# A layer of two decode attentions on one core: the first half of B's output weights loaded to 64 partitions in eight small transfers, and the last exp placed ahead of the product before it

## The chip, the cores and the metric

The kernel runs on one core of a Trainium2 chip. The metric is device time in microseconds (us), the median of three runs. One of the executions was taken by the hardware profiler; all rows and times below that are not called runs are from that one. Its times count from the first instruction of the span.

## What is computed

Two attention blocks, A and B, of the same shape, each for one query token. In each, a row x (512) is multiplied with wq (512 x 4096) to give 32 heads of 128; each head is scored against its own 8192 cached keys, goes through a softmax, and is multiplied with its 8192 cached values; the 32 results are laid end to end (4096) and multiplied with wo (4096 x 512). The two rows of 512 are put side by side.

```
q = (x @ wq).reshape(B, Sq, H, Dh).transpose(0, 2, 1, 3)
scores = einsum("bhqd,bhkd->bhqk", q, k_cache) * (Dh ** -0.5)
p = softmax(scores)
o = einsum("bhqk,bhkd->bhqd", p, v_cache)
y = o.transpose(0, 2, 1, 3).reshape(B, Sq, H * Dh) @ wo
out = concatenate([y of A, y of B], axis=-1)
```

All is bf16. The caches are 64 heads x 8192 x 128 x 2 bytes, twice: 268 MB. With wq and wo of both blocks (4 MB each) the kernel reads 285 MB.

## The kernel before

The work goes in **32 pairs of heads** (n = 0 to 31; 0 to 15 are A's, 16 to 31 B's). One pair has its two heads on 128 partitions: head one's 8192 positions on partitions 0 to 63, head two's on 64 to 127, 128 positions to a partition. So the keys of a pair are one transfer of 4 MB, 128 partitions x 32 KB, and so are the values.

`load_k` and `load_v` issue these transfers from SyncE's queue (SP) into two buffers each (`kn`, `vn`). A load into a buffer waits on SP until the pair that had it is through: keys of pair n wait for `red_done[n-2]`, values for `pv_done[n-2]`. The keys of pair 31 and the values of pair 31 come in four quarters.

For one pair: VectorE multiplies the keys with the query, in four pieces (`plan_mul`, L265). TensorE sums over the head dimension by 32 matmuls with an identity (`plan_red`, L274), VectorE adds the rest (`plan_sr`, L283) and takes each partition's maximum (`plan_max`, L289). `plan_gmax` brings the maxima into one row by a matmul (tile `mtp`, L295), and VectorE reduces them (L298). `plan_exp` spreads the maximum back to the partitions by four small matmuls (tile `bmp`, L308), and ScalarE makes `negb` of it (L312) and then the two exps (L319), which also leave the row sums. `plan_sum` adds the row sums by a matmul into the tile `misc` (L330; for the last three pairs L337) and takes the reciprocal. `plan_pv` multiplies with the values: 32 matmuls of 512 columns (L359), or, for the last three pairs (n >= MV = 29), 128 matmuls of 2 columns (L354), whose result `plan_o` scales straight into `oD` (L378).

The program's order is written out by hand: one Python loop over n calls these functions, and every engine carries out its own instructions in the order of the calls. In iteration n the steps of pair n up to its exp are mixed with the values product of pair n-2 (for the last three pairs, n-1).

**The output projection of B.** `oD` holds the heads with the head dimension on the partitions. `WOG` cuts the heads in groups; for each, `plan_relayout` (L414, L418, L420) turns the heads of the group into a layout in which partition p has rows of wo that lie side by side in memory, so that a group's part of wo is loaded in long runs: VectorE multiplies with a mask into `zb`, TensorE multiplies with `jsel` into `misc`, VectorE copies it out. `misc` is one tile, used in turn by the sums, by `plan_o` and by the relayouts; each use waits for the use before it. `plan_wot` (L441) then adds, for each group, four matmuls per row of wo, accumulating in `qyp`; `plan_yt` copies, transposes and casts the result (L454, L455, L457), and the last DMA writes it.

For B the groups are heads 0 to 15, 16 to 23, 24 to 27, 28 and 29, 30 and 31. The first, 2 MB on 128 partitions x 16 KB, is loaded in iteration 24. The other four, 2 MB together, are issued in iteration 31 behind the quarters of the values of pair 31, the last of the big transfers. All of wo lies in `wbuf`, which held wq and A's wo before.

```
            if n == 24:
                load_wo(1, 0)
            if n == NP - 1:
                for g in range(1, len(WOG[1])):
                    load_wo(1, g)
...
                plan_gmax(n)
                if ahead:
                    plan_mul(n + 1, 1)
                if n > MV:
                    plan_pv(n - 1, 0, T)
                plan_exp(n)
```

So in iteration 31 TensorE has, in this order: the matmuls of L295 for pair 31, the 128 matmuls of pair 30's values (L354), the matmuls of L308 for the exp of pair 31, the relayout product of heads 28 and 29 (L418), and from iteration 32 the sum of pair 31 (L337), the values product of pair 31 in four quarters, and the groups of the projection.

Of the kernel before, what the change touches and what calls it, by code (L numbers as in the profile page):

```python
# [6 lines left out]
ALU = mybir.AluOpType  # L7
AX = mybir.AxisListType
BF16 = mybir.dt.bfloat16
F32 = mybir.dt.float32  # L10

P = 128
# [11 lines left out]
class _Plan:  # L24
# [15 lines left out]
    def op(self, eng, fn, ctr=None, needs=(), inc=1):  # L40

        for m in needs:
            self.wait(eng, m)
        if ctr is None:
            self.prog[eng].append(fn)
            return None
        ctr.n += inc
        self.prog[eng].append(lambda e: fn(e).then_inc(ctr.sem, inc))
        return ctr, ctr.n


def bass_concat_heads__mha_block_cached__gqa_block_cached__decode_kernel(
# [17 lines left out]
    wos = [A_wo, B_wo]  # L70
    NA = 2
    H, Sk, Dh = ks[0].shape[1:]
    D = xs[0].shape[2]
    NOUT = wos[0].shape[1]
# [5 lines left out]
    T = Sk // HP  # L80
    assert T == 128
    PA = H // 2
    NP = NA * PA
    NK = NV = 2
# [3 lines left out]
    DW = 512 // HT  # L88
    assert Dh % DW == 0

    WOG = [[(0, 32)], [(0, 16), (16, 8), (24, 4), (28, 2), (30, 2)]]
    RG = [32, 16, 8, 4, 2]

    MV = NP - 3

    with ExitStack() as st:
# [3 lines left out]
        def sb(name, shape, dt):  # L100
            return ec(nc.sbuf_tensor(name, shape, dt))

        kn = sb("kn", [P, NK, T, Dh], BF16)
        vn = sb("vn", [P, NV, T, Dh], BF16)
        wbuf = sb("wbuf", [P, C * H * Dh], BF16)
        wq_sb = wbuf[:].rearrange("p (c n) -> p c n", c=C)
        wo_sb = wbuf[:].rearrange("p (j n) -> p j n", n=NOUT)
        qbc = sb("qbc", [P, NP, Dh], BF16)

        pt = sb("pt", [P, 2, T // 4, 8], BF16)  # L110
# [15 lines left out]
        rinv = sb("rinv", [P, NP, 2], F32)  # L126
        oD = sb("oD", [P, NA, H], BF16)
        zb = sb("zb", [P, 2, P], BF16)
        o2 = sb("o2", [P, NA, H], BF16)
        mask = {g: sb("mask%d" % g, [P, P // g], BF16) for g in RG}  # L130
        jsel = {g: sb("jsel%d" % g, [P, g], BF16) for g in RG}
        out_sb = sb("out_sb", [1, NOUT], BF16)
        NQ = NOUT // P
# [16 lines left out]
        def ctr(name):  # L150
            return _Ctr(nc, st, name)

        s_x = ctr("s_x")
        s_w = ctr("s_w")
        s_wo = [ctr("s_wo%d" % i) for i in range(5)]
        s_part = {(x, i): ctr("s_%s_part%d" % (x, i)) for x in "kv" for i in range(1, 4)}
        s_k = [ctr("s_k%d" % i) for i in range(NK)]
        s_v = [ctr("s_v%d" % i) for i in range(NV)]
# [4 lines left out]
        def dma(eng, dst, src, c, needs=()):  # L163
            return op(eng, lambda e: e.dma_start(dst, src), c, needs, inc=16)
# [50 lines left out]
            wq_in[a] = dma("SP", wbuf[:], wqs[a].rearrange("(p c) n -> p (c n)", p=P), s_w,  # L215
                           [q_done.get(a - 1)])

        def load_wo(a, g):
            h0, n = WOG[a][g]
            src = wos[a][h0 * Dh:(h0 + n) * Dh, :].rearrange("(p j) n -> p (j n)", p=P)  # L220
            wo_in[a, g] = dma("SP", wo_sb[:, h0:h0 + n, :].rearrange("p j n -> p (j n)"), src, s_wo[g],
                              [q_done[NA - 1] if a == 0 else wo_done[0]])


        for a in range(NA):
# [78 lines left out]
        def plan_exp(n):  # L304
            def bc(e):
                r = None
                for h in range(2):
                    r = e.matmul(bmp[:, 0:1], hrow[0:1, h, :], gm[0:1, n, h:h + 1],  # L308
                                 start=(h == 0), stop=(h == 1))
                return r  # L310
            m = op("PE", bc, c_pe, [i_pool, gm_done[n], nb_done.get(n - 1)])
            nb_done[n] = op("ACT", lambda e: e.activation(  # L312
                negb[:, n:n + 1], bmp[:, 0:1], AF.Copy, scale=-scale), c_act, [m])
            wait("ACT", nb_done[n])
            wait("ACT", pv_done.get(n - 2))
            wait("ACT", i_pool)
            for h in range(2):
                q = slice(h * HP, (h + 1) * HP)
                p_done[n] = op("ACT", lambda e, h=h, q=q: e.activation(  # L319
                    pt[q, n % 2, :, 4 * h:4 * h + 4],  # L320
                    s_sb[q, n % 2, :].rearrange("p (c t) -> p c t", t=4), AF.Exp,
                    bias=negb[q, n:n + 1], scale=scale, accum_out=rsum[q, n, h:h + 1]), c_act)
# [83 lines left out]
        o2_ready = {}  # L406

        def plan_relayout(a, g):
            h0, n = WOG[a][g]
            z = z_n[0] % 2  # L410
            z_n[0] += 1
            s = P // n
            zv = zb[:, z, :].rearrange("p (h s) -> p h s", s=s)
            m = op("DVE", lambda e: e.tensor_tensor(  # L414
                zv, oD[:, a, h0:h0 + n].unsqueeze(2).broadcast_to([P, n, s]),
                mask[n][:, None, :].broadcast_to([P, n, s]), ALU.mult),
                c_dve, [sel_ready[n], o_done[a * PA + (h0 + n) // 2 - 1], z_free.get(z)])
            z_free[z] = op("PE", lambda e: e.matmul(misc[:, 0:n], zb[:, z, :], jsel[n][:],  # L418
                                                    start=True, stop=True), c_pe, [m, misc_free[0]])
            o2_ready[a, g] = misc_free[0] = op("DVE", lambda e: e.tensor_copy(  # L420
                o2[:, a, h0:h0 + n], misc[:, 0:n]), c_dve, [z_free[z]])

        def plan_wo(g, j0, j1):

            def mm(e):
                r = None
                for j in range(j0, j1):
                    r = e.matmul(qyp[0:1, :], o2[:, 0, j:j + 1], wo_sb[:, j, :],  # L428
                                 start=(j == 0), stop=(j == H - 1))
                return r  # L430
            wo_done[0] = op("PE", mm, c_pe, [o2_ready[0, g], wo_in[0, g]] + ([qy_free[0]] if j0 == 0 else []))

        def plan_wot(g):

            h0, n = WOG[1][g]

            def mm(e):
                r = None
                for j in range(h0, h0 + n):
                    for i in range(NQ):  # L440
                        r = e.matmul(qyp[:, i:i + 1], wo_sb[:, j, i * P:(i + 1) * P],  # L441
                                     o2[:, 1, j:j + 1], start=(j == 0 and i == 0),
                                     stop=(j == H - 1 and i == NQ - 1), skip_group_check=True)
                return r
            wo_done[1] = op("PE", mm, c_pe, [o2_ready[1, g], wo_in[1, g], qy_free[0]])

        y_done = {}
# [17 lines left out]
        for n in range(NP + 1):  # L465
            last = n == NP

            ahead = n == NP - 2
            if n + 1 < NP:
                load_k(n + 1, 4 if ahead else 1)  # L470
            if 0 < n < NP:
                plan_sum(n - 1)
            if n < NP - 1:
                plan_mul(n, 0)
                plan_mul(n, 1)
            if 1 < n <= MV + 1:
                plan_pv(n - 2, 0, T)
                plan_ac(n - 2)
            if not last:
                load_v(n, 4 if n == NP - 1 else 1)  # L480
            if n == 0:
                load_wq(1)
            if n == 12:
                load_wo(0, 0)
            if n == 24:
                load_wo(1, 0)
            if n == NP - 1:
                for g in range(1, len(WOG[1])):
                    load_wo(1, g)
            if not last:  # L490
                plan_red(n, 0)
            if n < NP - 1:
                plan_mul(n, 2)
                plan_mul(n, 3)
            if not last:
                plan_sr(n, 0)
            if 1 < n <= MV + 1:
                plan_o(n - 2)
            if not last:
                plan_red(n, 1)  # L500
                plan_sr(n, 1)
                plan_max(n)
                if ahead:
                    plan_mul(n + 1, 0)
                plan_gmax(n)
                if ahead:
                    plan_mul(n + 1, 1)
                if n > MV:
                    plan_pv(n - 1, 0, T)
                plan_exp(n)  # L510
            else:
                plan_sum(n - 1)
                for i in range(4):
                    plan_pv(n - 1, i * T // 4, (i + 1) * T // 4)
                plan_wot(1)
            if n > MV:
                plan_o(n - 1)
            if 3 <= n < 7:
                plan_q(1, n - 3)
            if n == PA + 1:  # L520
                plan_relayout(0, 0)
            if PA + 1 < n <= PA + 5:
                plan_wo(0, 8 * (n - PA - 2), 8 * (n - PA - 1))
                if n == PA + 5:
                    plan_y()
            for g, (h0, k) in enumerate(WOG[1]):
                p = (h0 + k) // 2 + PA - 1
                if n == (p + 2 if p < MV - 1 else p + 1):
                    plan_relayout(1, g)
            if n == 28:  # L530
                plan_wot(0)
            if ahead:
                plan_mul(n + 1, 2)
                plan_mul(n + 1, 3)
        for g in range(2, len(WOG[1])):
            plan_wot(g)
        plan_yt()
        dma("SP", out[0, :, 0:NOUT], out_sb[:], s_out, [y_done[0]])
# [38 lines left out]
```

## Time and profile before

| what | value |
|---|---|
| runs before | 674.28 us median (674.13 to 674.54), three runs |
| the profiled execution | 674.46 us; its span 672.4 us |
| TensorE matmul busy | 554.5 us, 82% of the span |
| VectorE busy | 358.9 us, 53% |
| ScalarE busy | 63.6 us, 9% |
| read from HBM | 285.21 MB, 424 GB/s over the span |
| mean granted TensorE clock | 0.913 of full speed |

The profile is read in views. The page gives busy times, the span in 40 slices (with the busy share of the 16 DMA engines), the DMA queues, and groups of instructions. The chain of waits is followed back from the last instruction to what released each step. The timeline lists instructions with their starts, durations and the idle time before them. The windows give busy times between two moments. The trace behind the views also holds every DMA packet with its start, duration and size, and every semaphore event; where a number below is counted from these, the text says so.

### The profile page before, as it was taken

How to read it: one execution, taken by the hardware profiler on the slowest of the kernel's cores; microseconds unless marked ns; L12 is line 12 of the kernel's file. 1: busy time of each engine (PE TensorE's matmuls, PEld its weight loads, DVE VectorE, ACT ScalarE, POOL GpSimd, SP SyncE). 2: the span in 40 equal slices, each digit the busy share in tenths (PEclk: the TensorE clock that was granted, in tenths of full speed). 3: DMA queues.
4: the chain of work that ended last, by engine and by line, in shares of the span. 5: the costliest groups of instructions: out<-in, count | busy, mean ns of one | idle time of the engine just before them, and what ended most of it. 6: DMA issues, size and time to landing. Idle time of an engine off the chain costs nothing.

```text
span 672.4 us, 6851 instructions
## 1 busy us (share of the span) xinstructions
PE 554.5 (82%) x3006; PEld 233.2 (35%) x3006; DVE 358.9 (53%) x345; ACT 63.6 (9%) x200; POOL 2.6 (0%) x17
## 2 busy tenths in 40 slices
PE   2657799989888889874888899999889888798986
PEld 1223333333333333331333333333333333343345
DVE  1563456565455665615655556565545664456561
ACT  1101010111011001110110110111010111010000
POOL 1000000000000000000000000000000000000000
PEclk9969999898889998896898999988789988899876
DMA  9999999999999999999999999999999999999996
GB/s 374 437 436 433 432 425 424 435 434 433 432 432 425 432 435 432 431 428 437 425 430 434 431 430 435 430 427 434 426 433 436 431 426 431 430 433 434 415 423 256
DMA packets 11275, 285.65 MB, mean 425 GB/s; under 512 B 1259, under 2 KB 1262, under 8 KB 1646
## 3 DMA queue, kind: packets, MB, share of 16 engines
q1 hardware_dynamic: 11242, 285.22, 98.9%
q8 instruction: 23, 0.38, 0.2%
q14 instruction: 6, 0.05, 0.0%
q10 hardware_dynamic: 4, 0.00, 0.0%
HBM read 285.21 MB, written 0.00 MB: 424 GB/s over the span
## 4 chain that ended last, share of the span: by engine, by line
PE 57%; DMA 28%; DVE 9%; issue 3%; ACT 2%; SPq 0%
PE rps L274 26%; PE acc L359 24%; DMA kn<-in_A_k_cache_dram 16%; DMA kn<-in_B_k_cache_dram 8%; DVE kn L265 5%; DMA wbuf<-in_B_wo_dram 3%; DVE s_sb L283 2%; PE bmp L308 2%; ACT pt L319 2%; PE mtp L295 1%; PE qyp L428 1%; DVE m L289 1%; DVE gm L298 1%; PE misc L330 1%; PE misc L386 1%
## 5 line engine op out<-in xcount | busy, mean ns | idle before, releaser
L265 DVE TENSOR_TENSOR kn<-kn,qbc 128x4096 bf16<-128x4096 bf16 x128 | 284.7, 2284 | 84.2 <-DMA kn<-in_A_k_cache_dram 61.2
L274 PE MATMUL rps<-kn,ident 128*128 128x512 bf16 x1024 | 240.5, 390 | 24.2 <-DVE kn L265 24.2
L359 PE MATMUL acc<-vn,pt 128*8 128x512 bf16 x928 | 236.4, 419 | 0.0
L274 PEld LDWEIGHTS rps<-kn,ident 128*128 128x128 bf16 x1024 | 97.6, 100 | 152.2 <-issue 25.4
L359 PEld LDWEIGHTS acc<-vn,pt 128*8 128x8 bf16 x928 | 84.9, 93 | 137.5 <-issue 45.9
L283 DVE TENSOR_REDUCE s_sb<-rps 128x64 f32<-128x512 f32 x64 | 44.2, 691 | 126.5 <-PE rps L274 126.5
L371 ACT ACTIVATE accsb<-acc,rinv 8x512 bf16<-8x512 f32 x29 | 19.7, 678 | 244.5 <-PE acc L359 244.5
L295 PE MATMUL mtp<-ident_f,m 128*1 128x128 f32 x64 | 12.1, 271 | 35.3 <-DVE m L289 35.3
L334 DVE RECIPROCAL rinv<-misc 8x1 f32<-8x1 f32 x29 | 4.5, 155 | 64.9 <-PE misc L330 64.9
L312 ACT ACTIVATE negb<-bmp 128x1 f32<-128x1 f32 x32 | 5.5, 171 | 332.0 <-PE bmp L308 332.0
L330 PE MATMUL misc<-rsum,hind 128*8 128x1 f32 x116 | 7.2, 166 | 26.3 <-ACT pt L319 26.3
L308 PE MATMUL bmp<-gm,hrow 1*128 1x1 f32 x128 | 19.6, 253 | 11.2 <-DVE gm L298 11.2
L319 ACT ACTIVATE pt<-s_sb,negb 64x128 bf16<-64x128 f32 x64 | 25.5, 399 | 1.8
L308 PEld LDWEIGHTS bmp<-gm,hrow 1*128 1x128 f32 x128 | 16.9, 189 | 20.0 <-DVE gm L298 19.3
L295 PEld LDWEIGHTS mtp<-ident_f,m 128*1 128x1 f32 x64 | 2.7, 81 | 51.1 <-DVE m L289 51.1
L247 PE MATMUL qyp<-wbuf,xb 128*64 128x512 bf16 x64 | 13.7, 571 | 6.4 <-DMA wbuf<-in_A_wq_dram 4.3
L298 DVE TENSOR_REDUCE gm<-mtp 1x2 f32<-1x128 f32 x32 | 8.9, 278 | 14.6 <-PE mtp L295 14.6
L330 PEld LDWEIGHTS misc<-rsum,hind 128*8 128x8 f32 x116 | 4.8, 90 | 32.3 <-ACT pt L319 30.6
L319 ACT ACTIVATION_READ_ACCUMULATOR pt<-s_sb,negb 64x1 f32 x64 | 11.8, 185 | 0.0
L428 PE MATMUL qyp<-wbuf,o 128*1 128x512 bf16 x32 | 10.7, 494 | 0.0
L354 PEld LDWEIGHTS acc<-pt,vn 128*128 128x128 bf16 x384 | 10.3, 99 | 0.4 <-issue 0.4
L354 PE MATMUL acc<-pt,vn 128*128 128x2 bf16 x384 | 10.3, 164 | 0.0
(48 smaller groups left out, 65.6 us busy)
## 6 DMA issues: line engine op xcount, KB each, us to landing
kn<-in_A_k_cache_dram SPq DMA_DIRECT2D x16, 4096.0 KB, 26.1
vn<-in_A_v_cache_dram SPq DMA_DIRECT2D x16, 4096.0 KB, 23.7
kn<-in_B_k_cache_dram SPq DMA_DIRECT2D x15, 4096.0 KB, 25.5
vn<-in_B_v_cache_dram SPq DMA_DIRECT2D x15, 4096.0 KB, 23.0
wbuf<-in_A_wq_dram SPq DMA_DIRECT2D x1, 4096.0 KB, 12.3
wbuf<-in_B_wq_dram SPq DMA_DIRECT2D x1, 4096.0 KB, 30.3
wbuf<-in_A_wo_dram SPq DMA_DIRECT2D x1, 4096.0 KB, 32.6
kn<-in_B_k_cache_dram SPq DMA_DIRECT2D x4, 1024.0 KB, 21.2
```

The source lines that it names most:

```text
L265: mul_done[n, c] = op("DVE", lambda e: e.tensor_tensor(k, k, qbc[:, n:n + 1, :].broadcast_to([P, CT, Dh]), ALU.mult), c_mul, [k_in[n][c * ...
L274: r = e.matmul(rps[:, h, :].rearrange("p (t d) -> p t d", d=DW), ident[:], kn[:, n % NK, h * HT:(h + 1) * HT, i * DW:(i + 1) * DW], start= ...
L283: sr_done[n, h] = op("DVE", lambda e: e.tensor_reduce(s_sb[:, n % 2, h * HT:(h + 1) * HT], rps[:, h, :].rearrange("p (t d) -> p t d", d=DW ...
L295: m = op("PE", lambda e: e.matmul(mtp[0:1, 0:P], m1[:, n:n + 1], ident_f[:], start=True, stop=True), c_pe, [m_done[n], i_identf, gm_done.g ...
L298: gm_done[n] = op("DVE", lambda e: e.tensor_reduce(gm[:, n, :], mtp[0:1, 0:P].rearrange("o (h p) -> o h p", h=2), AX.X, ALU.max), c_dve, [m])
L308: r = e.matmul(bmp[:, 0:1], hrow[0:1, h, :], gm[0:1, n, h:h + 1], start=(h == 0), stop=(h == 1))
L319: p_done[n] = op("ACT", lambda e, h=h, q=q: e.activation(pt[q, n % 2, :, 4 * h:4 * h + 4], s_sb[q, n % 2, :].rearrange("p (c t) -> p c t", ...
L330: r = e.matmul(misc[0:8, 0:1], hind[:], rsum[:, n, h:h + 1], start=(h == 0), stop=(h == 1))
L354: r = e.matmul(acc[:, n % 2, 0:2], vn[:, n % NV, t, :], pt[:, n % 2, t // 4, t % 4:8:4], start=(t == 0), stop=(t == T - 1))
L359: r = e.matmul(acc[0:8, n % 2, :], pt[:, n % 2, c, :], vn[:, n % NV, 4 * c:4 * c + 4, :].rearrange("p t d -> p (t d)"), start=(c == 0), st ...
L371: ac_done[n] = op("ACT", lambda e: e.activation(accsb[:, n % 2, :], acc[0:8, n % 2, :], AF.Copy, scale=rinv[0:8, n, 0:1]), c_act, [pv_done ...
L428: r = e.matmul(qyp[0:1, :], o2[:, 0, j:j + 1], wo_sb[:, j, :], start=(j == 0), stop=(j == H - 1))
```

## The change

Five things are edited.

- **Groups of B.** Heads 0 to 15 become two groups. `WOG` now holds (first head, heads, rows of wo to a partition): heads 0 to 7 with 16 rows to a partition, which fill partitions 0 to 63, and heads 8 to 15 with 8 rows on 128 partitions. The four groups of the tail are as before.
- **Their loads.** Heads 0 to 7 (1 MB) are loaded by eight DMAs of 8 partitions x 16 KB each; DMA i takes the partitions b, b+4, ..., b+28 with b = 32*(i // 4) + i % 4. Two of the eight are issued in each of the iterations 22 to 25, behind the loads of that iteration. Heads 8 to 15 (1 MB, 128 partitions x 8 KB) follow in iteration 26. The load in iteration 24 is gone.
- **The tail's loads** are the same four transfers at the same place in SP's queue, but go into the `kn` buffer that pair 30's keys had, and wait for `red_done[30]` instead of `wo_done[0]`.
- **Relayout and projection** get one group more: one mask product, one matmul and one copy, and in iteration 28 a second `plan_wot` of 32 matmuls. The results `o2` are one tensor for each group.
- **The exp of pair 31** is called ahead of the values product of pair 30, so TensorE has L308 of pair 31 ahead of the 128 matmuls of L354 of pair 30. The iterations before keep their order.

```diff
-    WOG = [[(0, 32)], [(0, 16), (16, 8), (24, 4), (28, 2), (30, 2)]]
+    WOG = [[(0, 32, 32)], [(0, 8, 16), (8, 8, 8), (16, 8, 8), (24, 4, 4), (28, 2, 2), (30, 2, 2)]]
+        wo_kn = kn[:, NP % NK].rearrange("p t d -> p (t d)").rearrange("p (j n) -> p j n", n=NOUT)
...
-        def load_wo(a, g):
-            h0, n = WOG[a][g]
-            src = wos[a][h0 * Dh:(h0 + n) * Dh, :].rearrange("(p j) n -> p (j n)", p=P)
-            wo_in[a, g] = dma("SP", wo_sb[:, h0:h0 + n, :].rearrange("p j n -> p (j n)"), src, s_wo[g],
-                              [q_done[NA - 1] if a == 0 else wo_done[0]])
+        def wo_rows(a, g):
+
+            h0, n, r = WOG[a][g]
+            if a == 0 or g < 2:
+                return n * Dh // r, wo_sb, 16 if (a, g) == (1, 1) else 0
+            return P, wo_kn, h0 - WOG[1][2][0]
+
+        def load_wo(a, g, parts=range(8)):
+            h0, n, r = WOG[a][g]
+            np_, tile, j0 = wo_rows(a, g)
+            src = wos[a][h0 * Dh:(h0 + n) * Dh, :].rearrange("(p j) n -> p (j n)", p=np_)
+            dst = tile[0:np_, j0:j0 + r, :].rearrange("p j n -> p (j n)")
+            need = [q_done[NA - 1]] if a == 0 else [wo_done[0]] if g < 2 else [red_done[NP - 2]]
+            if np_ == P:
+                wo_in[a, g] = dma("SP", dst, src, s_wo[g], need)
+                return
+
+            for i in parts:
+                b = 32 * (i // 4) + i % 4
+                wo_in[a, g] = dma("SP", dst[b:b + 29:4, :], src[b:b + 29:4, :], s_wo[g], need)
...
-            if n == 24:
-                load_wo(1, 0)
+            if 22 <= n < 26:
+                load_wo(1, 0, range(2 * (n - 22), 2 * (n - 21)))
+            if n == 26:
+                load_wo(1, 1)
             if n == NP - 1:
-                for g in range(1, len(WOG[1])):
+                for g in range(2, len(WOG[1])):
                     load_wo(1, g)
...
-                if n > MV:
+                if n > MV and n < NP - 1:
                     plan_pv(n - 1, 0, T)
                 plan_exp(n)
+                if n == NP - 1:
+                    plan_pv(n - 1, 0, T)
             else:
                 plan_sum(n - 1)
                 for i in range(4):
                     plan_pv(n - 1, i * T // 4, (i + 1) * T // 4)
-                plan_wot(1)
+                plan_wot(2)
...
             if n == 28:
                 plan_wot(0)
+                plan_wot(1)
```

More of the change, by code (lines that the diff above doesn't have):

```diff
@@ L128, in bass_concat_heads__mha_block_cached__gqa_block_cached__decode_kernel @@
         zb = sb("zb", [P, 2, P], BF16)
-        o2 = sb("o2", [P, NA, H], BF16)
+        o2 = {(a, g): sb("o2_%d_%d" % (a, g), [P, r], BF16)
+              for a in range(NA) for g, (_, _, r) in enumerate(WOG[a])}
         mask = {g: sb("mask%d" % g, [P, P // g], BF16) for g in RG}
@@ L154, in bass_concat_heads__mha_block_cached__gqa_block_cached__decode_kernel @@
         s_w = ctr("s_w")
-        s_wo = [ctr("s_wo%d" % i) for i in range(5)]
+        s_wo = [ctr("s_wo%d" % i) for i in range(6)]
         s_part = {(x, i): ctr("s_%s_part%d" % (x, i)) for x in "kv" for i in range(1, 4)}
@@ L408, in plan_relayout @@
         def plan_relayout(a, g):
-            h0, n = WOG[a][g]
+            h0, n, r = WOG[a][g]
             z = z_n[0] % 2
             z_n[0] += 1
-            s = P // n
-            zv = zb[:, z, :].rearrange("p (h s) -> p h s", s=s)
+            w = P // r
+            m_ = n * w
+            zv = zb[:, z, 0:m_].rearrange("p (h s) -> p h s", s=w)
             m = op("DVE", lambda e: e.tensor_tensor(
[L415 to L418, printed above, removed]
+                zv, oD[:, a, h0:h0 + n].unsqueeze(2).broadcast_to([P, n, w]),
+                mask[r][:, None, :].broadcast_to([P, n, w]), ALU.mult),
+                c_dve, [sel_ready[r], o_done[a * PA + (h0 + n) // 2 - 1], z_free.get(z)])
+            z_free[z] = op("PE", lambda e: e.matmul(misc[0:m_, 0:r], zb[:, z, 0:m_], jsel[r][:],
                                                     start=True, stop=True), c_pe, [m, misc_free[0]])
             o2_ready[a, g] = misc_free[0] = op("DVE", lambda e: e.tensor_copy(
-                o2[:, a, h0:h0 + n], misc[:, 0:n]), c_dve, [z_free[z]])
+                o2[a, g][0:m_, :], misc[0:m_, 0:r]), c_dve, [z_free[z]])
         def plan_wo(g, j0, j1):
@@ L427, in mm @@
                 for j in range(j0, j1):
-                    r = e.matmul(qyp[0:1, :], o2[:, 0, j:j + 1], wo_sb[:, j, :],
+                    r = e.matmul(qyp[0:1, :], o2[0, g][:, j:j + 1], wo_sb[:, j, :],
                                  start=(j == 0), stop=(j == H - 1))
@@ L433, in plan_wot @@
         def plan_wot(g):
-            h0, n = WOG[1][g]
+            h0, n, r = WOG[1][g]
+            np_, tile, j0 = wo_rows(1, g)
+            end = g == len(WOG[1]) - 1
             def mm(e):
-                r = None
-                for j in range(h0, h0 + n):
+                res = None
+                for j in range(r):
                     for i in range(NQ):
[L441 to L444, printed above, removed]
+                        res = e.matmul(qyp[:, i:i + 1], tile[0:np_, j0 + j, i * P:(i + 1) * P],
+                                       o2[1, g][0:np_, j:j + 1], start=(g == 0 and j == 0 and i == 0),
+                                       stop=(end and j == r - 1 and i == NQ - 1), skip_group_check=True)
+                return res
             wo_done[1] = op("PE", mm, c_pe, [o2_ready[1, g], wo_in[1, g], qy_free[0]])
@@ L525, in bass_concat_heads__mha_block_cached__gqa_block_cached__decode_kernel @@
                     plan_y()
-            for g, (h0, k) in enumerate(WOG[1]):
+            for g, (h0, k, _) in enumerate(WOG[1]):
                 p = (h0 + k) // 2 + PA - 1
@@ L534, in bass_concat_heads__mha_block_cached__gqa_block_cached__decode_kernel @@
                 plan_mul(n + 1, 3)
-        for g in range(2, len(WOG[1])):
+        for g in range(3, len(WOG[1])):
             plan_wot(g)
```

## The prediction

> **What bounds the kernel now.** First the page's 40 slices: the busy share of the 16 DMA engines and the bytes per second.
>
> ```profile
> DMA  9999999999999999999999999999999999999996
> GB/s 374 437 436 433 432 425 424 435 434 433 432 432 425 432 435 432 431 428 437 425 430 434 431 430 435 430 427 434 426 433 436 431 426 431 430 433 434 415 423 256
> ```
>
> The transfers never pause; only the last slice falls, to 256 GB/s. PE at 82% is not the limit. Next the page's DMA queues:
>
> ```profile
> q1 hardware_dynamic: 11242, 285.22, 98.9%
> q8 instruction: 23, 0.38, 0.2%
> q14 instruction: 6, 0.05, 0.0%
> ```
>
> Beside the kernel's loads the DMA engines fetch instructions: 23 packets of 16 KB, 6 of 8 KB. Then the end of the chain of waits (start, us, what):
>
> ```profile
> 646.64 21.85 DMA wbuf<-in_B_wo_dram
> 668.49 0.05 issue
> 668.54 0.19 PE qyp L441
> 668.73 0.42 issue
> 669.14 0.57 PE qyp L441 x15
> ```
>
> The last link is a load of wo. By the semaphore events the last group is complete at 669.13, and the last 15 matmuls start at 669.14. So the end goes one to one with the last DMA engine to finish. The windows (PEclk, DMA share, GB/s are the last three columns) show that they do not finish together:
>
> ```profile
> 655.00:663.40 8.40, 6.19 (x167) 5.24 (x166) 2.04 (x7) 1.15 (x5) 0.00 (x0) 0.86 1.01 415
> 663.40:664.90 1.50, 1.50 (x61) 1.50 (x59) 0.00 (x0) 0.00 (x0) 0.00 (x0) 0.50 0.67 275
> 664.90:666.90 2.00, 1.63 (x61) 1.55 (x59) 0.45 (x2) 0.00 (x0) 0.00 (x0) 0.50 0.58 228
> 666.90:668.40 1.50, 1.30 (x46) 1.22 (x43) 0.16 (x1) 0.00 (x0) 0.00 (x0) 0.50 0.36 141
> ```
>
> From 663.4 on a third of the engines has nothing to do. I counted this from the trace's packets and semaphore events. Each 128-partition transfer leaves 16 events, one per engine. Those of the last transfer come, after the first one, at **0, 0.06, 0.15, 0.18, 0.20, 0.77, 1.45 | 3.04, 3.35, 3.37, 4.75, 4.78, 4.83, 4.96, 5.05, 5.20 us**: seven early engines, nine late. Followed back over the transfers, all run at one pace (9.70 us for eight packets of 32 KB); a lag comes from an instruction fetch and stays. Each of the 23 large fetches puts one engine 1.56 us back (at 50 us, from 0.41 to 1.97), in turns over the same eight engines. Small ones put one other engine back 0.97 us three times: that is the 3.04.
>
> The profile's execution took 674.46 us: 672.43 of span and 2.03 around it. The median is 0.18 lower; I make the sum on 674.46 and carry the difference to 674.28.
>
> **Part 1: heads 0 to 7 in eight DMAs of 8 partitions.** Bytes in total stay. A transfer of one partition (`out_sb`) left one data packet and one 4-byte packet, the one of four (`out_q`) four of each; so I take 8 partitions for 8 engines, one packet of 16 KB each. The eight DMAs all have the same form, so I take the same eight engines for all: they carry 8 x 0.614 us (median of 16 KB packets) for these heads, and, like all, 8 x 0.313 (8 KB) for heads 8 to 15. Before, each engine had 8 x 0.614 for heads 0 to 15. The eight **receivers** get 2.50 us and eight more 4-byte packets of 9 ns, **+2.57 us**; the other eight get 8 x 0.614 less, about **-2.40**.
>
> The time of the end is the largest lag. Eight receivers among seven early engines cannot all be early: at least one of the nine late ones receives. The best choice is the one at 3.04: it ends at 3.04 + 2.57 = 5.61 where the worst was 5.20, **+0.41 us**. The six that now end at 4.75 to 5.20 go to 2.35 to 2.80 and no longer matter; the worst engine is another one, no better. If a receiver at 3.37 joins, +0.74. If one at 5.20 does, +2.57. Which eight receive? The one-partition `out_sb` ran at 663.46, just behind the earliest engine's last packet of wo, so that small-transfer engine is one of the six without fetches. This speaks for the receivers being the eight engines without large fetches, and the late one among them that at 3.04. I take +0.41.
>
> [...] The slices above show queues that never run dry, so I hold that the other eight engines go on with the next transfer.
>
> What it issues: eight instructions on SP instead of one, at 0.43 us each (the row of the wo loads), and one for heads 8 to 15: two per iteration, 0.86 us. Behind them on SP is the next load of keys, which waits for `red_done` anyway: pair 29's was issued at 579.06 and its packets began at about 590 on the earliest engine. These 11 us of queue hide it (8 for the values of pair 28, issued at 591.47, begun at 599.7); without them it would cost 0.86 us an iteration. The wait for `wo_done[0]` is over by iteration 22.
>
> Iteration 28 gets 32 matmuls more, 0.85 us (64 took 1.69 on the chain), and one more relayout (VectorE 0.27 + 0.17, PE 0.18). The engines wait for keys there (VectorE is idle 2.6 us before pair 28's product, 2.2 before pair 29's, both released by the DMA), and the same 8 to 11 us of queue cover it. The tail's loads into `kn` wait for `red_done[30]`, done before `pv_done[29]`, which SP has already waited for: nothing. PE fetches some 66 instructions more, 4 KB, a quarter of a fetch: the fetches come a little earlier, on engines that now have 2.4 us to spare.
>
> **Part 2: the exp ahead.** Rows of the timeline before:
>
> ```profile
> 657.05 3.37 PE L354 MATMUL acc<-pt,vn 128*128 128x2 bf16 x128
> 657.16 0.28 DVE L298 TENSOR_REDUCE gm<-mtp 1x2 f32<-1x128 f32 x1 [0.47 <-PE mtp L295]
> 660.35 0.60 PE L308 MATMUL bmp<-gm,hrow 1*128 1x1 f32 x4
> 660.46 0.16 DVE L378 TENSOR_TENSOR oD<-acc,rinv 128x2 bf16<-128x2 f32 x1 [3.02 <-PE acc L354]
> 661.00 0.19 PE L418 MATMUL misc<-jsel,zb 128*128 128x2 bf16 x1
> 661.22 0.16 DVE L420 CAST o<-misc 128x2 bf16<-128x2 f32 x1 [0.28 <-PE misc L418]
> 662.25 0.59 PE L337 MATMUL misc<-rsum,ones_f 128*128 128x2 f32 x2 [1.06 <-ACT pt L319]
> 662.69 3.59 PE L354 MATMUL acc<-pt,vn 128*128 128x2 bf16 x128
> ```
>
> Now L308 runs from 657.48 to 658.08, pair 30's product to about 661.4, and the exp (1.85 us from L308 to L337) is done beside it. But what is late next is the relayout of heads 28 and 29: it starts when that product ends and takes 0.96 us to its copy (660.42 to 661.38 above), and L337 must wait for this copy, as it writes the same `misc`. So L337 starts at about 662.42 and pair 31's product at 662.86 instead of 662.69: **0.17 us later**, not earlier. Between ends: if the relayout did not hold it up, it would come 0.8 us earlier. Either way the loads cover it: the values' last quarter lands by 664.6, heads 16 to 23 at 667.0, the last group at 669.54. PE alone would reach the end of its last matmuls at 667.90 + 32 x 0.032 = 668.9 against 669.71, so 0.8 us of cover. Cost 0.
>
> **Sum:** 674.46 + 0.41 = 674.87, against the median **674.7 us**.
>
> **Rivals.**
> - *Forecast, 0.71:* the end moves by the engine at 3.04 or 3.37, 674.6 to 675.1.
> - *A twice or thrice delayed fetch engine is among the receivers, 0.15:* slower. Place: the last wo transfer; price up to 2.57, 676.9; it passes 0.2% (1.35 us) from the point at which a receiver's lag before was over 3.98, and six of sixteen engines were. For: only one receiver can be told from the trace. Against: that one has no fetches, and eight fetch engines leave just eight others.
> - *The eight DMAs are spread over all 16 engines, 0.06:* the change doesn't do what it says; every engine has what it had, 674.4. Against: the packets of `out_q`.
> - *The lag of the 3.04 engine goes, 0.08:* its small fetches fall elsewhere, and DMA ends 2 us earlier. Then PE's chain ends it: 0.8 less the 0.17, 673.7; if the exp comes 0.8 earlier as well, 672.9 or less. Against: the fetches follow instruction counts that hardly change.
>
> **Numbers.** Faster by over 0.2% (under 672.93): half of the last case, 0.04. Slower by over 0.2% (over 675.63): 0.15. Within 0.2%, about what a measurement of this kernel can tell from no change: 0.71 + 0.06 + 0.04 = 0.81. The range takes in the forecast, the even spread, the milder half of the last case and 0.4 us beyond the slower bound for what I have not seen, 673.4 to 676.0; the fetch engine among the receivers stays outside.
>
> **What would show it.** In the trace after: the eight DMAs leave 64 packets of 16 KB; the last transfer's lags have six at about 2.6, the six now at 4.75 to 5.20 at about 2.5, one alone at about 5.6. L308 of pair 31 ahead of L354 of pair 30; L337 ends its wait on the copy of L420. The DMA share of the last 5 us higher than 0.36 to 0.67 up to one engine's tail. Wrong if the last lag is under 4.5 (a worst engine relieved) or over 6.5.

## The result and the profile after

The changed kernel takes **676.32 us** (median of nine runs, 676.05 to 676.82), the kernel before 674.52 (nine runs, 674.13 to 675.31). The ratio is 1.0027, with a 95% interval of 1.0016 to 1.0037: **1.8 us slower**. The forecast was 674.7, no change that can be told; the range ended at 676.0. The case that came true is the rival I gave 0.15.

The profiled executions took 676.55 against 674.46 us, their spans 674.7 against 672.4. The slices and queues of the changed kernel:

```profile
DMA  9999999999999999999999999999999999999995
GB/s 373 435 434 435 432 431 427 433 428 428 430 434 433 424 435 428 433 432 431 431 427 432 431 432 433 430 431 432 427 430 427 433 432 428 436 430 427 419 416 208
```

```profile
q1 hardware_dynamic: 11370, 285.22, 98.6%
q8 instruction: 24, 0.39, 0.2%
q14 instruction: 6, 0.05, 0.0%
```

Bytes and rate are what they were; there is one large fetch more, at 671.3, when the loads are all but done. The last slice is 48 GB/s lower (208 in the place of 256), the others differ by at most 9. Around it, the windows (last columns: granted clock, DMA share, GB/s):

```profile
655.00:663.40 8.40, 6.93 (x133) 4.80 (x132) 1.53 (x4) 1.15 (x5) 0.00 (x0) 0.82 0.99 412
663.40:664.90 1.50, 0.75 (x23) 0.58 (x19) 0.59 (x3) 0.00 (x0) 0.00 (x0) 0.50 0.80 314
664.90:666.90 2.00, 1.83 (x55) 1.86 (x56) 0.19 (x2) 0.00 (x0) 0.00 (x0) 0.50 0.58 226
666.90:668.40 1.50, 1.50 (x63) 1.50 (x60) 0.00 (x0) 0.00 (x0) 0.00 (x0) 0.50 0.27 101
668.40:670.00 1.60, 1.58 (x54) 1.44 (x52) 0.45 (x2) 0.00 (x0) 0.00 (x0) 0.50 0.16 63
670.00:671.50 1.50, 1.22 (x34) 0.97 (x31) 0.16 (x1) 0.00 (x0) 0.00 (x0) 0.50 0.13 44
```

The share falls, and then stays for three microseconds at 0.16 and 0.13: at first three, and from 669.6 on two engines of sixteen (0.125) are still at work. The end of the chain of waits (start, us, what):

```profile
650.33 21.21 DMA kn<-in_B_wo_dram
671.53 0.14 issue
671.67 0.37 PE qyp L463 x8
```

The last group of wo is complete at 671.53; it was 669.12, as the events show. The sixteen events of the last transfer (first one, then the lags behind it, us):

```
before 663.93 | 0 .06 .16 .18 .20 .77 1.46 | 3.04 3.36 3.37 4.75 4.78 4.83 4.96 5.05 5.20
after  663.36 | 0 .29 1.29 1.34 3.02 3.04 3.05 3.18 3.20 3.37 3.61 3.84 4.59 | 6.26 8.12 8.18
```

Two engines, at 8.12 and 8.18, set the end. Over the small transfers eight engines moved 4.9 us back against the other eight. Right behind them the lags were 0, 0.11, 2.9 and more: two early engines are not among the receivers, and two of the latest are.

PE's last chain is 2.4 us later as well: the matmuls of the maxima of pair 31 start at 659.10 (below), and started at 656.74 before:

```profile
656.74 0.38 PE L295 MATMUL mtp<-ident_f,m 128*1 128x128 f32 x2 [1.10 <-DVE m L289]
```

The keys of pair 31 are not the reason. By the events their last quarter is complete at 646.97 (before 644.50), and VectorE starts on the last two quarters at 647.75 (before 645.48) without waiting for a load. In the chain of waits no load stands between 587 and 646; PE's own work does. Its part in iteration 28, two lines before and two after:

```profile
601.19 1.69 PE qyp L441 x64
603.05 8.62 PE acc L359 x32
```

```profile
601.91 2.70 PE qyp L463 x96
604.79 9.14 PE acc L378 x32
```

0.7 us are there when these matmuls of the projection start, behind the keys of pair 28 (VectorE starts on them at 586.87, before at 585.87). The 32 matmuls more take 1.0 us. The values product behind them takes 0.5 more: by the trace's clock records 4.4 us of it ran at a granted clock of 0.5, before 3.4. At the end PE is through with the matmuls before the last eight at 671.32, 0.21 us ahead of the last load:

```profile
670.30 1.02 PE L463 MATMUL qyp<-o,kn 128*128 128x1 bf16 x24
671.67 0.35 PE L463 MATMUL qyp<-o,kn 128*128 128x1 bf16 x8 [0.35 <-DMA kn<-in_B_wo_dram]
```

The early exp, in the timeline of the changed kernel:

```profile
659.10 0.38 PE L314 MATMUL mtp<-ident_f,m 128*1 128x128 f32 x2 [1.10 <-DVE m L308]
659.85 0.60 PE L327 MATMUL bmp<-gm,hrow 1*128 1x1 f32 x4 [0.37 <-DVE gm L317]
660.38 3.58 PE L373 MATMUL acc<-pt,vn 128*128 128x2 bf16 x128
664.54 0.18 PE L438 MATMUL misc<-jsel,zb 128*128 128x2 bf16 x1 [0.58 <-DVE zb L434]
664.76 0.16 DVE L440 CAST o<-misc 128x2 bf16<-128x2 f32 x1 [0.28 <-PE misc L438]
665.07 0.56 PE L356 MATMUL misc<-rsum,ones_f 128*128 128x2 f32 x2 [0.34 <-DVE o L440]
665.49 3.57 PE L373 MATMUL acc<-pt,vn 128*128 128x2 bf16 x128
```

L356 (L337 before) is released by the copy of the relayout, L440, as forecast. From the matmul of the maxima to pair 31's values product it is 6.39 us (659.10 to 665.49); it was 5.95 (656.74 to 662.69). The step that was to shorten this way made it 0.44 longer.

### The profile page after: what moved, and what is told of

It reads as the page before. It is cut to its first block, busy times and chain, and to the rows that moved or that the text cites. A ratio compares the mean times of both kernels' runs of the same rounds, so it can differ in the third digit from the quotient of the medians.

```text
span 674.7 us, 6928 instructions
## 1 busy us (share of the span) xinstructions
PE 555.3 (82%) x3039; PEld 233.9 (35%) x3039; DVE 359.1 (53%) x347; ACT 63.6 (9%) x200; POOL 2.6 (0%) x17
## 4 chain that ended last, share of the span: by engine, by line
PE 48%; DMA 36%; DVE 10%; issue 4%; ACT 2%; SPq 1%
PE rps L293 23%; DMA kn<-in_A_k_cache_dram 20%; PE acc L378 20%; DMA kn<-in_B_k_cache_dram 12%; DVE kn L284 7%; DMA kn<-in_B_wo_dram 3%; DVE s_sb L302 2%; PE bmp L327 1%; ACT pt L338 1%; PE mtp L314 1%; DVE m L308 1%; PE qyp L448 1%; DVE gm L317 1%; SPq L168 1%; PE misc L349 1%
## 5 line engine op out<-in xcount | busy, mean ns | idle before, releaser
L378 PE MATMUL acc<-vn,pt 128*8 128x512 bf16 x928 | 239.1, 423 | 0.0
L266 PE MATMUL qyp<-wbuf,xb 128*64 128x512 bf16 x64 | 12.1, 514 | 6.4 <-DMA wbuf<-in_A_wq_dram 4.3
L308 DVE TENSOR_REDUCE m<-s_sb 128x1 f32<-128x128 f32 x32 | 9.2, 286 | 1.1
```

Of the source, the lines that this page charges most:

```text
L308: m_done[n] = op("DVE", lambda e: e.tensor_reduce(m1[:, n:n + 1], s_sb[:, n % 2, :], AX.X, ALU.max), c_dve, [sr_done[n, 1]])
L378: r = e.matmul(acc[0:8, n % 2, :], pt[:, n % 2, c, :], vn[:, n % NV, 4 * c:4 * c + 4, :].rearrange("p t d -> p (t d)"), start=(c == 0), st ...
```

## The experiments

Three theories. **U**, uneven engines: the 64 KB more went to some engines that were late already. **E**: the early exp costs it. **S**: eight small transfers cost a fixed time, whatever engines they use. Line numbers are those of each kernel. "Base" below is the kernel of the first run, which has all of the change but the small DMAs and the 32 matmuls more (heads 0 to 7 take 64 matmuls on 64 partitions, and 32 on 128).

**One large transfer again (base).**

```diff
-    WOG = [[(0, 32, 32)], [(0, 8, 16), (8, 8, 8), (16, 8, 8), (24, 4, 4), (28, 2, 2), (30, 2, 2)]]
+    WOG = [[(0, 32, 32)], [(0, 8, 8), (8, 8, 8), (16, 8, 8), (24, 4, 4), (28, 2, 2), (30, 2, 2)]]
...
-            if 22 <= n < 26:
-                load_wo(1, 0, range(2 * (n - 22), 2 * (n - 21)))
+            if n == 24:
+                load_wo(1, 0)
```

> The changed kernel with one part undone: heads 0 to 7 of B come in one transfer of 128 partitions x 8 KB in iteration 24; the sixth group, the loads into kn and the early exp stay. Theory U (uneven engines: the 64 KB more on eight engines fall on some that instruction fetches already put back, so the keys of pair 31 and the last of wo land 2.4 us later): back to 674.5 to 675.0, lags of the last transfer 0 to 5.2 us again. Rival E (the early exp, with its new wait for the relayout of heads 28 and 29, costs the time): stays at 676.0 to 676.4. Rival S (eight small transfers cost a fixed time each, whatever engines they use): 674.5 to 675.0 as well; this run does not tell U from S.

Measured: 674.54 us (674.3 to 675.12), ratio to before 0.9999 (0.9990 to 1.0008). The last lag is 5.17. So the whole loss hangs on heads 0 to 7 on 64 partitions: on their small DMAs, or on the 32 matmuls more that go with them. E falls here.

**The early exp alone**, in the kernel before:

```diff
-                if n > MV:
+                if n > MV and n < NP - 1:
                     plan_pv(n - 1, 0, T)
                 plan_exp(n)
+                if n == NP - 1:
+                    plan_pv(n - 1, 0, T)
```

> The kernel before with the early exp of pair 31 alone. Theory U: 674.3 to 675.0, since PE's last chain gets up to 0.44 us later (5.94 us from the maxima's matmul to pair 31's values product before, 6.38 in the changed kernel) but the last wo transfer covers it. Rival E: 676.0 to 676.4. Rival S: as U.

Measured: 674.68 us, ratio 1.0004 (0.9995 to 1.0013): nothing that can be told, and no gain.

**The small DMAs without the early exp** (the edit above undone in the changed kernel):

> The changed kernel with the exp of pair 31 back at its old place. Theory U: 676.0 to 676.4, the lags of the last transfer up to 8.2 us as in the changed kernel. Rival E: 674.5 to 675.0. Rival S: as U.

Measured: 676.24 us, ratio 1.0026 (1.0017 to 1.0034); the last two lags are 7.36 and 7.38 behind a first event at 663.78, so the last group lands at 671.16. The early exp takes no part in the 1.8 us.

**The small DMAs cut in two**, to number the engines:

```diff
-                wo_in[a, g] = dma("SP", dst[b:b + 29:4, :], src[b:b + 29:4, :], s_wo[g], need)
+                k = i % 4 + 1
+                for j0_, j1_ in ((0, k), (k, 8)):
+                    lo, hi = b + 4 * j0_, b + 4 * (j1_ - 1) + 1
+                    wo_in[a, g] = dma("SP", dst[lo:hi:4, :], src[lo:hi:4, :], s_wo[g], need)
```

> The changed kernel with each of its eight DMAs of 8 partitions cut in two: 1 and 7 partitions, 2 and 6, 3 and 5, 4 and 4, and the same once more. If a DMA of k partitions goes to the same first k engines each time, eight engines get 16, 14, 12, 10, 6, 4, 2 and 0 packets of 16 KB, and the others none; the lags then rise between iterations 22 and 25 by 9.8, 8.6, 7.4, 6.1, 3.7, 2.5, 1.2 and 0 us against the others, which tells which lag belongs to which engine. Theory U: the time follows the engine that comes out last, from 676 if the most loaded engines have no fetches (lag 0.1 + 9.8 - 2.4 is still over 5.2) to 681 if they have. Rival S: sixteen transfers in the place of eight cost twice as much, 678, and the lags of all engines rise alike. Rival E: 676.5.

Measured: 683.97 us (one run), over all I had expected, and the lags could not be numbered: packets of 16 KB now took 0.61 to 1.50 us. Why, this run does not show. This asked for the next two runs.

**Stairs**: the eight DMAs as they were, and seven unread loads more, for which the kernel also waits at its end.

```diff
             if n == 26:
                 load_wo(1, 1)
+                for i in range(7):
+                    b = 32 * (i // 4) + i % 4
+                    hi = b + 4 * (6 - i) + 1
+                    extra = dma("SP", wo_sb[b:hi:4, 24:32, :].rearrange("p j n -> p (j n)"),
+                                wos[1][0:8 * Dh, :].rearrange("(p j) n -> p (j n)", p=64)[b:hi:4, 0:8 * NOUT],
+                                s_ex, [wo_done[0]])
```

> The changed kernel with seven loads more in iteration 26, whose data nobody reads: DMAs of 7, 6, 5, 4, 3, 2 and 1 partitions x 8 KB, each on the first of the partitions that the eight small DMAs use, so that engine number 0 of the eight gets seven packets more and number 7 none, 0.32 us a packet. It reads 0.23 MB more. Theory U with small DMAs on the same first k engines: the lags of the eight receivers rise by 2.25, 1.93, 1.61, 1.29, 0.97, 0.64, 0.32 and 0 us on top of the 4.9 against the other eight, which numbers them. The time is 676.3 to 676.7 if the two receivers with three large fetches are the last two of the eight, and up to 678.5 if they are the first two. Each 16 KB packet stays at 0.61 us. Rival S (a fixed cost of each small DMA, which all engines pay): 676.3 + 7/8 of 1.8 = 677.9, and no stairs in the lags.

Measured: 677.13 us (one run). The 16 KB packets took 0.614 us on average (0.611 to 0.622). Over iteration 26 the lags of the eight receivers went from 4.71, 4.78, 4.83, 4.90, 6.24, 7.95, 8.07, 8.08 to 4.83, 6.35, 6.46, 6.91, 8.11, 8.25, 8.68, 9.31; the eight others stayed but for one large fetch (584.8 us). I fitted all orders of the stairs to these, with 0.62 us for one small instruction fetch that fell into that stretch (in the kernel before, the one at 650.7 us put an engine from 0.15 to 0.77). In every close fit the three receivers at 7.95 to 8.08 are **engines 3, 5 and 6**, and 0, 1, 2, 4 and 7 are early ones. This is a fit, not a reading; the two runs with unread loads below test it.

For the two receivers with large fetches the trace's packets give a reading as well. By their lengths the large fetches repeat in eights (1.10, 1.09, 1.02, 1.02, 1.07, 1.07, 1.06, 1.10 us in the kernel before), as one would expect of eight engines in turn. In the changed kernel the lags of the two late receivers step up by about 1.5 us at two packets of 1.02, at 607.0 and 628.8, and without the early exp at 551.9 and 587.2: the two are neighbours in the turn. At which engine the turn begins differs between the traces. In every trace in which all eight receivers got more, both have had three fetches by the end; a turn that leaves both at two is not among them.

**The other half of the partitions**: heads 0 to 7 on partitions 64 to 127.

```diff
-                wo_in[a, g] = dma("SP", dst[b:b + 29:4, :], src[b:b + 29:4, :], s_wo[g], need)
+                up = wo_sb[64 + b:64 + b + 29:4, 0:r, :].rearrange("p j n -> p (j n)")
+                wo_in[a, g] = dma("SP", up, src[b:b + 29:4, :], s_wo[g], need)
```

(The relayout and the matmuls of the group move to partitions 64 to 127 too.)

> The changed kernel with heads 0 to 7 on partitions 64 to 127 in place of 0 to 63; all else the same. Which engines run a DMA of 8 partitions? If the DMA's shape decides (always the same first eight), the same engines receive, the lags show 0 and 0.1 us for two early ones again, and their packets now go to the other half of the partitions, as some did in the run with the cut DMAs, where 16 KB took 0.61 to 1.50 us: 677 or more. If the partitions decide, the other eight engines receive, six of them with large fetches, the packets take 0.61 us, and the time is 676.3 to 677.0, with six early engines at 0 to 0.9 us.

Measured: 688.06 us (one run). Behind the small DMAs the lags begin with 0 and 0.35 and then jump to 3.1, as in the changed kernel: the same engines receive. The third fetches of 1.02 us (659.4, 675.7) step the lags of two of the latest here too. So here the form of the DMA decided the engines, not the partitions. The packets of the cut DMAs, which the expectation names beside these, did not go to that half: by that edit all of them wrote partitions 0 to 63. The price surprised me. The windows of this kernel, before, over and behind the small DMAs:

```profile
440.00:480.00 40.00, 37.26 (x171) 14.93 (x171) 21.66 (x20) 3.66 (x12) 0.00 (x0) 0.91 1.01 432
490.00:560.00 70.00, 55.44 (x255) 22.32 (x254) 34.86 (x34) 6.17 (x19) 0.00 (x0) 0.93 1.00 377
580.00:620.00 40.00, 32.29 (x230) 14.58 (x231) 20.61 (x21) 2.98 (x11) 0.00 (x0) 0.89 1.01 431
```

and the middle one in the changed kernel:

```profile
490.00:560.00 70.00, 58.53 (x271) 23.78 (x269) 36.72 (x38) 6.08 (x21) 0.00 (x0) 0.93 1.01 433
```

The engines are as busy as ever (1.00), but move 377 in the place of 433 GB/s: their packets take longer (those of 32 KB 1.38 us in the place of 1.22).

**Unread loads on three engines, and on eight**, added to the base; nothing is taken off any engine, and the kernel also waits for them at its end. (The edit for three; for eight, the 2 is a 7.)

```diff
             if n == 26:
                 load_wo(1, 1)
+                for i in range(8):
+                    b = 32 * (i // 4) + i % 4
+                    hi = b + 4 * 2 + 1
+                    extra = dma("SP", wo_sb[b:hi:4, 24:32, :].rearrange("p j n -> p (j n)"),
+                                wos[1][0:8 * Dh, :].rearrange("(p j) n -> p (j n)", p=P)[b:hi:4, :],
+                                s_ex, [wo_done[0]])
```

> The kernel with heads 0 to 7 in one 128-partition transfer (674.54 us) and eight loads more in iteration 26 whose data nobody reads: 3 partitions x 8 KB each, on engines 0, 1 and 2 by the order found in the run with the stairs. Each of the three gets eight packets more, 2.57 us; 0.20 MB in all. Theory U: these three end at 0 to 1.5 us of lag, so they have room: 674.4 to 674.9, no slower. Rival B (what counts is the number of bytes, at 432 GB/s): +0.46, 675.0. Rival S (what counts is the number of small DMAs, 1.8 us for eight): 676.3.

> The same with eight loads more of 8 partitions x 8 KB, so engines 0 to 7 get eight packets more each, 2.57 us; 0.52 MB in all. Nothing is taken off the other eight. Theory U: engines 3, 5 and 6 are late ones, two of them with three large fetches; the end moves by 2.2 to 2.6, to 676.8 to 677.2, although only 0.52 MB are added. Rival B: +1.2, 675.7. Rival S: 676.3, as in the run with 3 partitions.

Measured: on three engines 674.56 us, ratio 1.0001 (0.9992 to 1.0009); on eight 676.74, ratio 1.0035 (1.0022 to 1.0049). Both have eight more DMAs, and each engine that they use has eight packets more. On engines 0 to 2 they are free; with 3 to 7 among them they cost 2.2 us, while 0.52 MB at 432 GB/s would be 1.2. S falls, a cost by bytes falls, U stands. As in the base, heads 0 to 7 take 32 matmuls here, so the 2.2 us come without the 32 more.

**More instruction fetches**, in the base:

```diff
                 plan_exp(n)
+                if 4 <= n < 12:
+                    def fill(e):
+                        for _ in range(64):
+                            e.matmul(mtp[:, 300:301], ident[:], ident[:, 0:1], start=True, stop=True)
+                    op("PE", fill)
```

> The kernel with heads 0 to 7 in one 128-partition transfer and, in iterations 4 to 11, 64 matmuls of one column more on PE, whose result nobody reads: 1024 instructions, 64 KB, four large instruction fetches more (27 or 28), and 1.7 us of PE in each of eight iterations, which wait for loads. Tests whether the fetches make the lags. Theory F (they do): the engines that are fourth in turn get 1.56 us more before the end, so the last lag is 6.4 to 6.8 instead of 5.2, and the time is 675.7 to 676.2. Rival (the lags come from the engines themselves, or the fetches only mark them): 674.5, lags as before.

Measured: 675.78 us, ratio 1.0018 (1.0010 to 1.0027), the last three lags 6.26, 6.31 and 6.36 us, just short of F's 6.4 to 6.8. The page of this kernel:

```profile
q8 instruction: 27, 0.44, 0.3%
```

Four fetches of 16 KB more than the 23 of the kernel before, for 1024 instructions, issued in iterations in which PE waits for loads and hundreds of microseconds ahead of the end, and the kernel is 1.2 us later than the base. The fetches make the lags, and the lag makes the time.

**Twice the dose**: heads 8 to 15 by small DMAs as well.

```diff
-    WOG = [[(0, 32, 32)], [(0, 8, 16), (8, 8, 8), (16, 8, 8), (24, 4, 4), (28, 2, 2), (30, 2, 2)]]
+    WOG = [[(0, 32, 32)], [(0, 8, 16), (8, 8, 16), (16, 8, 8), (24, 4, 4), (28, 2, 2), (30, 2, 2)]]
...
-            if n == 26:
-                load_wo(1, 1)
+            if 26 <= n < 30:
+                load_wo(1, 1, range(2 * (n - 26), 2 * (n - 25)))
```

(Its part of the projection moves to iteration 30.)

> The changed kernel with heads 8 to 15 as well on 64 partitions by eight DMAs of 8 partitions x 16 KB, in iterations 26 to 29, and their part of the projection in iteration 30. Engines 0 to 7 get 8 x 0.614 us in the place of 8 x 0.313, the others nothing. Theory U: the late receivers come out 2.4 us later, 678.5 to 679.0. Rival S (fixed cost of the eight small DMAs): +1.8, 678.1. If the time does not move, the receivers are not what bounds.

Measured: 678.56 us, ratio to before 1.0059 (1.0045 to 1.0072), the last two lags 11.02 and 11.04. Against the changed kernel that is 2.24 us more; 2.4 was U's step, and S's 1.8 is not far enough from it to be told by this run alone.

No version that I tried beats the kernel before. Engines 0 to 2 have room, but the unread loads show only that filling it costs nothing; a version that takes data off the late engines by way of these three was not tried. By the lags above, an estimate, it could gain some tenths of a microsecond, and an interval here is 1.2 us wide.

## Why the prediction was wrong

- **The bound.** Right: the end follows the last DMA engine, and the lags come from instruction fetches (with four more of them, the run with filled-in matmuls, the last lag was 6.36 us where the base had 5.17).
- **The size.** Right: the receivers moved 4.9 us back against the other eight, where 2.57 + 2.40 = 4.97 was forecast. The last group landed 2.41 later (669.12 to 671.53). The six latest engines were at 4.75 to 5.20; one of them as a receiver gives 2.12 to 2.57 (4.75 + 2.57 - 5.20 = 2.12). The span grew by 2.3, the median by 1.8.
- **Which engines receive.** This is the step that failed: "This speaks for the receivers being the eight engines without large fetches, and the late one among them that at 3.04." The eight receivers are the same each time (the run on partitions 64 to 127), but two of the engines with three large fetches are among them, and two early engines are not. They end at 8.12 and 8.18, where the prediction had one engine alone at about 5.6. From one known engine I had concluded on a tidy pattern of two halves. My own count spoke against it: I took one receiver as known, the engine of `out_sb`, which was an assumption, and six of the other fifteen engines were over 3.98. Had the other seven been drawn from these fifteen by chance, none of the six would be among them in 36 of 6435 draws. The slower rival, which I had priced at up to 2.57 us, needed only one of them. A weight of 0.71 on the pattern had only the row of that one engine behind it, and the range was closed on that side for the same reason.
- **The 32 extra matmuls.** "The engines wait for keys there" was read from VectorE; PE, which got the matmuls, does not wait there. They took 1.0 us, not 0.85, and with the product behind them put PE's chain 1.5 us back; the cover at the end is 0.35 us, not 0.8. This did not make the 1.8 us: the last load still ends later than PE, and the unread loads on eight engines cost 2.2 us without these matmuls. But the term was not nothing. An estimate, which no run shows: with the receivers as forecast, PE alone would have ended at 668.9 + 1.5 + 0.3 (the exp, below) = 670.7, 1.0 behind the 669.71 before, and the kernel at about 675.3 instead of 674.7.
- **SP, the relayout, the loads into `kn`:** cost nothing, as said: the base has the sixth group and the `kn` loads, and takes 674.54; with eight more DMAs on SP it takes 674.56.
- **The early exp.** The mechanism was right (the relayout of heads 28 and 29 is late next); the size was 0.44 us, not 0.17. Of the 0.27 missed, 0.21 is pair 30's product, 3.58 us in the place of 3.37: the granted clock was 0.5 from 660.36 on, and before, the product ran at 1.0. With the early exp alone the product took 3.41, and the stretch 6.22 (655.39 to 661.61), 0.27 longer than before. Without effect on the time.
- **The other eight engines.** That they go on with the next transfer was right: while the small DMAs ran (490 to 560 us) the changed kernel moved 433 GB/s at a DMA share of 1.01. That the eight DMAs use the same eight engines agrees with the run on partitions 64 to 127, and by the fit of the stairs DMAs of fewer partitions use the first of these; no row shows the chip's engine numbers.

## What to carry to other kernels

In a kernel that transfers all the time, look at when each DMA engine finishes, not at their mean (here two set the end at 8.12 and 8.18 us, and thirteen of sixteen were done by 4.59): work moved between engines pays only if none of the receivers is among the late ones, and an unread load on a few engines is a cheap way to find out which are which (here 674.56 us with three engines and 676.74 with eight). Instructions are transfers too: here TensorE's fetches sat on eight of the DMA engines, 1.56 us of lag for each large one, and pushed the end. A wait of one engine need not cover work on another (here VectorE's 2.6 us did not cover the 1.0 us more on PE): look for the wait on the engine that gets the work. And where a gain hangs on an identity that no row shows, count how many of the possible choices give it before weighing it.

## What the runs showed that I had not expected

- **A large instruction fetch costs more than its bytes.** 16 KB of wo were 0.614 us of one engine. A fetch packet of 16 KB took 1.02 to 1.10 us in the kernel before, the engine's lag grew by 1.56 us for each, and 1024 instructions more made the kernel 1.2 us slower.
- **Loads to the other half of the partitions took longer.** When the eight DMAs went to partitions 64 to 127, on the same engines, their 16 KB packets took 1.04 us on average (0.66 to 1.29) in the place of 0.614, and the 32 KB packets of all transfers from 480 to 570 us 1.38 in the place of 1.22; 267 of 999 were over 1.25. That is (64 x 0.42 + 999 x 0.157) / 16 = 11.5 us per engine, and the kernel was 11.7 us slower than the changed one. No run here shows why.
- **Two engines ran dry by being too early.** In the changed kernel the two early engines were 2.9 us ahead of the third behind the small DMAs, and 1.3 us at the last transfer: by then they had waited for work. By the trace's packets 16 are under way at a time up to 646.1 us and again from 647.4, but 14 from 646.4 to 647.1; in the kernel before it is 16 from 643 to 652. The loads of pair 31's values are issued behind pair 29's product, at 646.17 (before 643.90); 1.5 of these 2.3 us come from iteration 28, with its 32 matmuls more. The late engines had work enough: between the transfers whose first events are at 646.70 and 650.81 their lag fell from 10.02 to 8.40, so they took 2.5 us for that 1 MB, as elsewhere.
